# Second added exponential copies made on GpSimd as 32-bit additions, with planner limits every 20 units

## The chip, the cores and the metric

The kernel runs on one core of a Trainium2 chip. The metric is device time in microseconds: 1727.33 us is the median of three runs (1726.25 to 1729.32). The engines are called as in the profile: PE is TensorE's matrix multiplication and PEld its weight loads, DVE is VectorE, ACT is ScalarE, POOL is GpSimd, and SP issues the DMAs.

## The reference

Four attention layers in a row on x of 2048 tokens and 512 features, each with a layer norm ahead and a residual behind; the weights of the A layers are the same both times, and so are those of the B layers. There are 32 heads of 16 features.

```python
x = x + A(layernorm(x), wq, wk, wv, wo, beta)
x = x + B(layernorm(x), wqkv, wo)
x = x + A(layernorm(x), wq, wk, wv, wo, beta)
x = x + B(layernorm(x), wqkv, wo)

# B: full attention over all 2048 keys
scores = einsum('bhqd,bhkd->bhqk', q, k) * Dh ** (-0.5)
o = einsum('bhqk,bhkd->bhqd', softmax(scores), v) @ wo

# A: four segments of 512 tokens; causal attention inside a segment, and a memory of the earlier ones
p = softmax(q_s @ k_s.T * scale + mask); a_dot = p @ v_s
a_mem = (phi(q_s) @ M) / (phi(q_s) @ z + 1e-6)          # phi(t) = t + 1 if t > 0 else exp(t)
out_s = g * a_mem + (1 - g) * a_dot                     # g = sigmoid(beta)
M += phi(k_s).T @ v_s;  z += sum(phi(k_s))
```

## The kernel before

All of x stays in SBUF. The matrix of scores is never whole: a bank of PSUM (128 partitions by 512 float32) takes the scores of 128 keys against 512 queries of one head, and the exponential of the bank goes to SBUF as bf16. It is the weight of the next matmul (A layers) or its moving data (most of the B layers, called flipped: 17 columns of V and ones against 512 queries). The seventeenth column sums the exponentials, so that the normalisation comes after the PV product.

Work is a list of units. In each unit `unit` (L1650) issues the QK matmuls of three banks, or of two, and one ScalarE exponential over all of them (L1727, 1536 or 1024 elements per partition). Where a unit has only two banks for ScalarE, one or two more banks are given to VectorE: these are the taken banks (`dx_pick`, L1172). Every matmul goes through `mm` (L577), so the profile shows most of TensorE's work under that line.

VectorE makes its exponentials by arithmetic on bit patterns. `dx_first` (L1240, instruction at L1248) scales the scores from PSUM, adds a bias, and writes them as 16-bit integers, whose bits are then read as bf16. Two more copies of these codes, shifted by 36 and 84 (`EXP_STEPS`), are made from the first: the three values enter PV one after the other, and their sum approximates the exponential better than one. The added copies are instructions from SBUF to SBUF: `task_dx` (L1286) makes them over two banks, 1024 codes, at L1302; `dx_four` (L1309) does the same over four banks, 2048 codes, at L1319. The buffers are `dxt`, and KA, QA, VA, wA and wB once their own contents are no longer needed (`dx_buf`, L1196). That is why a copy appears in the profile as `VA<-KA` or `wB<-wB`.

Each taken bank therefore has three PV products in place of one. `pv_taken` (L1906) picks which of them TensorE issues after a unit, and `pv_phase` (L1926) issues them.

No order is left to the hardware: every engine has a queue that the program builds with its own clocks. `Sched.estimate` (L128) gives each instruction a planned end on its engine's clock from its inputs and a fixed duration; the planner compares these clocks (for example `late`, L1331) to decide whether to take a bank, when to run a background task (projections, layer norms, memory updates, the added copies), and what TensorE issues next. `held` and `PORT` there model that a VectorE operation from SBUF to SBUF waits for a GpSimd operation in progress. The limits of these decisions are class attributes of `Builder`; `PLAN` (L362) holds rows that replace some of them, one row for each stretch of `STRETCH` = 40 units (`set_limits`, L1972).

GpSimd's queue has, in the same planned order: the masking of diagonal blocks of the A layers (L1741), the multiplication that leaves one parity of heads in the queries (`qm`, L1617, `select` at L1575), the product by the reciprocal of the sums (`ob`, L1874, `divide` at L1864), some normalised x (`xn`, L777), and memsets. PSUM has eight banks: two slots of three for the units, and two for sums and background work.

Keep-warm matmuls with zeros are added to TensorE's list where it would otherwise be idle (`keep_busy`, L557, and `fill_gap`, L581).

Of the kernel before, what the change touches and what calls it, by code (L numbers as in the profile page):

```python
# [5 lines left out]
dt = mybir.dt  # L6
ACT = mybir.ActivationFunctionType
ALU = mybir.AluOpType

P = 128  # L10
# [77 lines left out]
class Sched:  # L88
# [4 lines left out]
    def __init__(self):  # L93
        self.ops = {e: [] for e in ENGS}
        self.t = {e: 0.0 for e in ENGS}
        self.tiles = []

        self.streams, self.cover = [], 0.0
        self.recent, self.over, self.pe_end, self.floor = [], [0.0, 0.0], 0.0, 0.0
        self.held, self.port, self.raw = [], False, False  # L100
        self.pe_seen, self.pe_no, self.pe_at = {}, [0], [0.0]
# [26 lines left out]
    def estimate(self, op, ns, gap, tile):  # L128
# [19 lines left out]
        elif e == "sp":  # L148
            st = max(ready, self.t[e])
            self.t[e] = st + max(gap, 600)  # L150
            op.end = st + ns
        else:
            op.end = max(self.t[e] + gap, ready + ns)
            if e == "pool":
                self.held = self.held[-7:] + [(op.end - ns, op.end)]
            elif self.port:
                for a, z in self.held:
                    if a + 20 < op.end - ns < z - PORT:
                        op.end = z - PORT + ns
            self.t[e] = op.end  # L160
# [198 lines left out]
class Builder:  # L359
    STRETCH = 40  # L360
# [3 lines left out]
        1: dict(ACT1=400, R_LATE=1200, DX_BANK=700, NEAR=18, FILL_DVE=400, BACK=3, CR_W=1900, CR_B=1800, R_PAIRS=2, PAIRS=24, DIV_LATE=800, DVE_LATE=800),  # L364
        2: dict(MARGIN=500, DX_BANK=900, NEAR=8, SLACK=550, EARLY=300, FILL=0.42, CR_B=1200, PART=3, NEARW=20, PAIRS=60, BUSY_WAIT=500, DX_FIN=3000, POOL_QM=1, POOL_XN=1),
        3: dict(ACT1=600, NEAR=8, TAKEN_A=1, SLACK=550, PV_SKIP=900, FILL_DVE=200, BACK=8, CR_W=1900, NEARW=20, OPART=2, TAKEN=0.4, LOW=14, DVE_LATE=800, QWAIT=8, HOLD_AT=40, PHI_LATE=0),
        4: dict(R_LATE=1200, NEARW=40, PAIRS=24, MASK_PE=800, LEVEL=3, TAKEN=0.5, LOW=30),
        5: dict(R_LATE=1500, DX_LATE=900, REST=12, NEAR=8, TAKEN_A=1, R_NEAR=50, PV_SKIP=500, FILL_DVE=400, BUSY_ROOM=900, CR_W=1300, DX_LAG=1, LOW=20, HOLD_SEGS=2),
        6: dict(ACT1=600, NEAR=10, PV_SKIP=200, DX_LAG=3, MASK_PE=800, LEVEL=3, DIV_LATE=2500, BG_BANK=100, QUAD=0),
        7: dict(ACT1=400, REST=16, NEAR=3, SLACK=350, R_NEAR=10, EARLY=0, FILL_DVE=200, BUSY_ROOM=300, CR_B=1800, R_PAIRS=2, PAIRS=999, TAKEN=0.3, QWAIT=8, QMIN=3, HOLD_AT=12, LN1_AT=6),  # L370
# [12 lines left out]
        20: dict(MARGIN=600, DX_LATE=900, EVAC_ACT=300, SLACK=550, PV_SKIP=100, CR_B=1200, R_PAIRS=2, MASK_PE=800, DIV_LATE=2500, BUSY_WAIT=500, GAP=1, BG_BANK=100, QWAIT=3, QMIN=3, HOLD_AT=40, LN1_AT=6, BUSY_BACK=800),
        21: dict(FILL_DVE=200, BACK=10, FILL=0.53, CR_W=1300, CR_B=1800, CR_A=1700, CARRY_W=0, NEARW=20, LEVEL=3, BG_BANK=400, QMIN=1, HOLD_MAX=0),
        22: dict(ACT1=200, DX_LATE=500, NEAR=10, PV_SKIP=200, EARLY=500, FILL=0.53, CR_B=1800, CARRY_W=1500, OPART=2, DX_LAG=1, MASK_PE=800, LEVEL=3, DIV_LATE=800, DVE_LATE=800, BG_BANK=100, QUAD=0, LN1_AT=6),
        23: dict(R_LATE=1200, R_NEAR=50, FILL_DVE=200, BACK=8, CR_A=1200, NEARW=40, OPART=4, PAIRS=999, LEVEL=3, TAKEN=0.25, QUAD=0, QMIN=4, HOLD_SEGS=2),
        24: dict(R_LATE=1500, DX_LATE=900, EVAC_ACT=100, REST=12, NEAR=8, TAKEN_A=1, SLACK=250, R_NEAR=50, PV_SKIP=100, EARLY=500, FILL_DVE=200, CR_W=1300, CR_A=1200, DX_LAG=1, LOW=20, BG_BANK=100, POOL_QM=1),
        25: dict(ACT1=300, MARGIN=600, R_LATE=2200, EVAC_ACT=1500, NEAR=18, CR_W=1900, CR_B=1800, R_PAIRS=2, DX_LAG=1, PAIRS=999, DIV_LATE=800, TAKEN=0.5, DVE_LATE=800, BG_BANK=400, PHI_LATE=300),
        26: dict(MARGIN=500, DX_LATE=700, REST=10, SLACK=350, EARLY=500, FILL_DVE=200, BUSY_ROOM=300, BACK=8, CR_W=1500, R_PAIRS=2, PAIRS=24, DIV_LATE=800, TAKEN=0.3, BG_BANK=100, QWAIT=8, QMIN=4, LN1_AT=6),
        27: dict(MARGIN=800, DX_BANK=700, REST=4, NEAR=10, SLACK=350, EARLY=500, FILL_DVE=200, BUSY_ROOM=300, BACK=8, CR_W=1500, PART=1, R_PAIRS=2, PAIRS=24, TAKEN=0.3, BG_BANK=100, QWAIT=8, QMIN=4, LN1_AT=6),  # L390
        28: dict(EVAC_ACT=800, NEAR=5, SLACK=350, R_NEAR=10, BACK=6, CARRY_W=400, NEARW=40, OPART=3, PAIRS=60, DIV_LATE=2500, BUSY_WAIT=0, TAKEN=0.3, DVE_LATE=800, BUSY_BACK=800),
        29: dict(DX_BANK=900, SLACK=700, PV_SKIP=100, EARLY=100, FILL_DVE=200, BUSY_ROOM=300, BACK=10, FILL=0.47, CR_W=1500, PART=3, R_PAIRS=2, TAKEN=0.3, DVE_LATE=800, LN1_AT=3, BUSY_BACK=800),
        30: dict(ACT1=300, MARGIN=800, REST=12, SLACK=700, PV_SKIP=100, EARLY=100, BACK=6, FILL=0.42, CR_W=1500, CARRY_W=400, PART=3, R_PAIRS=2, MASK_PE=800, DIV_LATE=2500, DVE_LATE=800, QWAIT=3, HOLD_MAX=0),
        31: dict(DX_LATE=700, DX_BANK=700, REST=20, PV_SKIP=100, BUSY_ROOM=900, FILL=0.57, CR_A=1700, PART=3, R_PAIRS=2, OPART=4, DX_LAG=3, MASK_PE=800, BUSY_WAIT=500, TAKEN=0.3, DVE_LATE=800, BG_BANK=100, QMIN=4, DX_FIN=3000),
# [891 lines left out]
    def task_dx(self):  # L1286
        while True:
# [18 lines left out]
            for i, (g, what, r) in enumerate(ents):  # L1306
                self.dxq.append((self.step + self.DX_LAG, g, what, r, b, i, [0]))
# [821 lines left out]
```

## Time and profile before

| | before |
|---|---|
| median of the runs | 1727.33 us (1726.25 to 1729.32, 3 runs) |
| span of the profiled execution, first to last instruction | 1724.4 us |
| ACT busy | 1696.4 us, 98% |
| PE busy | 1606.1 us, 93% |
| DVE busy | 1515.5 us, 88% |
| POOL busy | 211.3 us, 12% |
| granted TensorE clock, mean | 1.000 |

A group in the profile is named by line, engine, operation and tiles (`out<-in`, with the numbers of the buffers left out), then shapes and count, total busy time, mean duration of one in ns, and the idle time before it with what ended it. In a view by stretches each engine has its busy time in that stretch and, in brackets, its instructions; after the engines come the granted clock, the DMA share and GB/s. In a timeline the columns are start, duration, engine, line, operation. A row of waits reads: us in total, times, longest. Where one line of the program is shown alone, three durations are the shortest, median and longest one in ns.

### The profile page before, as it was taken

The numbers are of one execution on the slowest core, as the hardware profiler recorded it, in microseconds if no ns is written. First come the engines' busy times: TensorE is split into PE (matmuls) and PEld (weight loads), VectorE is DVE, ScalarE is ACT, GpSimd is POOL, SyncE is SP. The second block draws the span as 40 slices with busy tenths as digits, with TensorE's granted clock in tenths as the row PEclk, the third lists the DMA queues.
The fourth block names the chain that finished last, engine by engine and source line by source line (L and its number), as shares of the span: only waits on it lengthen the run. The fifth ranks groups of instructions, "written<-read, shape, count | busy, mean of one in ns | idle before, by whom it ended". The sixth has DMA issues, their size and how long they took to land.

```text
span 1724.4 us, 44750 instructions
## 1 busy us (share of the span) xinstructions
PE 1606.1 (93%) x19458; PEld 573.9 (33%) x19531; DVE 1515.5 (88%) x2928; ACT 1696.4 (98%) x1595; POOL 211.3 (12%) x321
## 2 busy tenths in 40 slices
PE   8898899999999899999999999999999999999999
PEld 4553435322222523522234222532222222222226
DVE  6757675999998789899886999889999999999997
ACT  8899999999999999999999999999999999999998
POOL 3211301111100402100002000110011000000000
PEclk9999999999999999999999999999999999999999
DMA  6110201000112131102112111011011000000000
GB/s 178 39 20 19 43 15 34 6 14 14 29 24 55 33 93 32 33 10 59 44 23 33 47 44 38 8 34 37 10 23 38 10 13 14 19 10 17 16 14 18
DMA packets 148421, 54.42 MB, mean 32 GB/s; under 512 B 128768, under 2 KB 147712, under 8 KB 148224
## 3 DMA queue, kind: packets, MB, share of 16 engines
q1 hardware_dynamic: 148224, 51.56, 13.9%
q8 instruction: 153, 2.51, 0.6%
q14 instruction: 44, 0.36, 0.1%
HBM read 18.88 MB, written 2.10 MB: 12 GB/s over the span
## 4 chain that ended last, share of the span: by engine, by line
ACT 77%; PE 16%; DVE 4%; issue 1%; POOL 1%; DMA 1%; another core or an unknown queue 0%; SPq 0%; ACTq 0%
ACT pT L1727 76%; PE ps L577 16%; ACT amem L844 1%; DVE lnst L748 1%; DVE KA L1248 0%; POOL xn L777 0%; DMA xT<-xn 0%; DVE wB L1248 0%; DMA tb<-ub 0%; DVE VA L639 0%; DVE lnst L750 0%; DVE KA L639 0%; DVE dxt L1248 0%; POOL qm L1617 0%; DVE wA L1248 0%
## 5 line engine op out<-in xcount | busy, mean ns | idle before, releaser
L1727 ACT ACTIVATE pT<-ps 128x1024 bf16<-128x1024 f32 (+1 forms) x1549 | 1664.6, 1280 | 15.5 <-PE ps L577 12.8
L577 PE MATMUL ps<-qm,KB 32*128 32x512 bf16 x4096 | 557.2, 384 | 78.1 <-ACT pT L1727 63.0
L577 PE MATMUL ps<-pT,VB 128*17 128x512 bf16 x2909 | 494.2, 384 | 2.0 <-DVE KA L1248 0.5
L577 PEld LDWEIGHTS ps<-qm,KB 32*128 32x128 bf16 x4096 | 143.4, 91 | 602.2 <-ACT pT L1727 515.1
L1248 DVE TENSOR_SCALAR KA<-ps 128x512 uint16<-128x512 f32 (+1 forms) x413 | 291.6, 723 | 11.2 <-PE ps L577 9.4
L1248 DVE TENSOR_SCALAR dxt<-ps 128x512 uint16<-128x512 f32 (+1 forms) x325 | 230.9, 721 | 14.0 <-PE ps L577 12.0
L577 PE MATMUL ps<-dxt,VB 128*17 128x512 bf16 x993 | 217.8, 381 | 0.0
L577 PEld LDWEIGHTS ps<-pT,VB 128*17 128x17 bf16 x2909 | 115.6, 87 | 285.2 <-issue 271.9
L1874 POOL TENSOR_TENSOR ob<-tb,rd 128x512 bf16<-128x512 bf16 x31 | 33.9, 1092 | 798.2 <-DVE rd L1870 798.2
L1248 DVE TENSOR_SCALAR wA<-ps 128x512 uint16<-128x512 f32 (+1 forms) x169 | 119.9, 723 | 2.3 <-PE ps L577 1.4
L577 PE MATMUL ps<-QA,VB 128*17 128x512 bf16 x420 | 117.8, 381 | 0.0
L1741 POOL TENSOR_SCALAR_AFFINE_SELECT pT<-pT 128x256 bf16<-128x256 bf16 (+4 forms) x128 | 67.4, 541 | 410.2 <-ACT pT L1727 410.2
L577 PE MATMUL ps<-woB,zero 128*32 128x512 bf16 (+1 forms) x347 | 115.1, 381 | 0.2 <-issue 0.2
L577 PE MATMUL ps<-VA,VB 128*17 128x512 bf16 x420 | 113.8, 381 | 0.0
L577 PE MATMUL ps<-wA,VB 128*17 128x512 bf16 x534 | 113.1, 381 | 0.0
L577 PE MATMUL ps<-qm,KA 32*128 32x128 bf16 (+2 forms) x1536 | 92.7, 254 | 18.0 <-ACT pT L1727 13.9
L1617 POOL TENSOR_SCALAR qm<-QB,par 128x512 bf16<-128x512 bf16 x98 | 79.0, 816 | 229.1 <-PE ps L577 215.8
L577 PE MATMUL ps<-VA,pT 128*128 128x51 bf16 (+1 forms) x2540 | 103.2, 187 | 1.8 <-DVE ob L1824 0.7
L577 PE MATMUL ps<-KA,VB 128*17 128x512 bf16 x420 | 100.7, 381 | 0.0
L577 PEld LDWEIGHTS ps<-VA,pT 128*128 128x128 bf16 x2540 | 88.7, 96 | 20.4 <-issue 7.7
L1302 DVE TENSOR_SCALAR dxt<-dxt 128x1024 uint16<-128x1024 uint16 (+1 forms) x216 | 85.7, 420 | 1.2
L1248 DVE TENSOR_SCALAR wB<-ps 128x512 uint16<-128x512 f32 (+1 forms) x108 | 84.1, 791 | 1.8 <-PE ps L577 0.8
(167 smaller groups left out, 1929.6 us busy)
## 6 DMA issues: line engine op xcount, KB each, us to landing
wB<-in_B_wqkv_dram SPq DMA_DIRECT2D x48, 128.0 KB, 2.3
wA<-in_A_wk_dram SPq DMA_DIRECT2D x16, 128.0 KB, 2.2
wA<-in_A_wq_dram SPq DMA_DIRECT2D x16, 128.0 KB, 2.3
wA<-in_A_wv_dram SPq DMA_DIRECT2D x16, 128.0 KB, 2.4
out_dram<-x SPq DMA_DIRECT2D x8, 256.0 KB, 2.2
x<-in_A_x_dram SPq DMA_DIRECT2D x3, 512.0 KB, 9.5
wB<-in_B_wqkv_dram SPq DMA_DIRECT2D x1, 1536.0 KB, 12.7
oT<-ob SPq DMA_TRANSPOSE x63, 2.5
```

Source lines behind the costliest of these rows:

```text
L577: self.sc.add("pe", lambda e: e.matmul(out, lhsT, rhs, start=start, stop=stop, skip_group_check=True), reads=reads, banks=[(bank, "w", all ...
L748: self.op("dve", (lambda i, t: lambda e: e.bn_stats(st[:, k, i, 0:6], self.x[:, t, :]))(i, t), reads=[self.b_x[t]], writes=[bs], ns=690, p ...
L844: self.op("act", lambda e: e.activation(et, src, ACT.Exp), reads=bsrc, writes=self.b_amem, ns=1023, gap=915)
L1248: self.op("dve", lambda e: e.tensor_scalar(d, o, SCALE * LOG2E * 128, 127.0 * 128 + EXP_BIAS, op0=ALU.mult, op1=ALU.add), writes=self.b_dx ...
L1302: self.op("dve", (lambda d, s, c: lambda e: e.tensor_scalar(d, s, float(c), None, op0=ALU.add))(d, s, c), reads=self.b_dxs[b][0:len(ents)] ...
L1617: self.op(eng, (lambda m, q, col: lambda e: e.tensor_scalar(m, q, col, 0.0, op0=ALU.mult, op1=ALU.add))(m, q, col), reads=[bq, self.b_par] ...
L1727: self.sc.add("act", (lambda dst, src: lambda e: e.activation(dst, src, ACT.Exp, scale=SCALE))(dst, src), writes=self.b_pT[slot * 3 + i:sl ...
L1741: self.op("pool", (lambda blk, pat: lambda e: e.affine_select(blk, blk, pattern=pat, compare_op=ALU.is_ge, fill=0.0, base=0, channel_multi ...
L1874: self.op(eng, lambda e: e.tensor_tensor(ob, t[:, :, :, 0:16], rb, ALU.mult), reads=[br] + self.b_tb, writes=self.b_ob[oi], **(dict(ns=125 ...
```

## The change

- The second added copy (shift 84) may be made by GpSimd. `pool_copy` views source and destination as 32-bit integers, two codes in each, and adds 84 × 65537, which shifts both halves by 84. The addend is one number per partition, in the new tile `shift`, read 512 times. Four banks at once become two such additions. The instruction depends on the source codes and on VectorE's first added copy of the same codes. It is put on GpSimd when GpSimd's planned clock is at most `POOL_C` (300) ns ahead of VectorE's; otherwise VectorE makes the copy as before.
- `dx_late` lets TensorE's list skip a PV product whose GpSimd copy is planned to come more than `POOL_WAIT` (100) ns after TensorE's clock. The product stays in the list for a later unit.
- The planned clock of GpSimd now also waits for VectorE operations from SBUF to SBUF in progress (`taken`).
- `STRETCH` is 20 in place of 40, and `PLAN` has 78 rows in place of 40, with other values.

```diff
     def estimate(self, op, ns, gap, tile):
...
             if e == "pool":
+                for a, z in self.taken:
+                    if a < op.end - ns + 20 < z:
+                        op.end = z - 20 + ns
                 self.held = self.held[-7:] + [(op.end - ns, op.end)]
             elif self.port:
                 for a, z in self.held:
                     if a + 20 < op.end - ns < z - PORT:
                         op.end = z - PORT + ns
+                self.taken = self.taken[-15:] + [(op.end - ns, op.end - 60)]
...
 class Builder:
-    STRETCH = 40
+    STRETCH = 20
     PLAN = {
...
+    POOL_C, POOL_NS, POOL_WAIT = 300, 2, 100
...
+        self.shift = sb("shift", [P, 1], dt.int32)
...
+        pool(lambda e: e.memset(self.shift[:, :], EXP_STEPS[1] * 65537), [self.b_shift])
...
     def task_dx(self):
...
                 d = self.dx_buf(b, k + 1)[:, 0:w]
+                if k and self.pool_copy(d, s, self.b_dxs[b][0:len(ents)], [self.b_dxt[b][k + 1]], self.b_dxt[b][k]):
+                    continue
...
+    def pool_copy(self, d, s, src, dst, first, now=False):
+
+        if not now and (not self.POOL_C or self.sc.t["pool"] > self.sc.t["dve"] + self.POOL_C):
+            return False
+        d, s = d.bitcast(dt.int32), s.bitcast(dt.int32)
+        n = 512 if len(src) == 2 else 256
+        c = bcast(self.shift[:, 0:1], [[0, n]])
+        self.op("pool", lambda e: e.tensor_tensor(d, s, c, ALU.add), reads=src + [first, self.b_shift], writes=dst, ns=150 + self.POOL_NS * n, gap=130 + self.POOL_NS * n)
+        self.cr_dve += 350
+        return True
...
     def dx_four(self, pairs):
...
+            d = self.dx_buf(b, k + 1, 2)
+            if k and self.pool_copy(d[:, 0:1024], s[:, 0:1024], self.b_dxs[b], [self.b_dxt[b][k + 1]], self.b_dxt[b][k]):
+                self.pool_copy(d[:, 1024:2048], s[:, 1024:2048], self.b_dxs[b + 1], [self.b_dxt[b + 1][k + 1]], self.b_dxt[b + 1][k], True)
+                self.cr_dve += 350
+                continue
             self.cr_dve -= 250
...
     def pv_taken(self, g, now, used=()):
...
             for ent in ents:
+                if not now and self.dx_late(ent):
+                    continue
                 if ent[6][0] <= len(EXP_STEPS) and loads[ent[3]] < level:
...
+    def dx_late(self, ent):
+
+        k, slot = ent[6][0], ent[4]
+        w = self.b_dxt[slot][k].last_write if 0 < k <= len(EXP_STEPS) else None
+        return w is not None and w.eng == "pool" and w.end + LAG["pool"] > self.sc.t["pe"] + self.POOL_WAIT
```

More of the change, by code (lines that the diff above doesn't have):

```diff
@@ L99, in __init__ @@
         self.recent, self.over, self.pe_end, self.floor = [], [0.0, 0.0], 0.0, 0.0
-        self.held, self.port, self.raw = [], False, False
+        self.held, self.taken, self.port, self.raw = [], [], False, False
         self.pe_seen, self.pe_no, self.pe_at = {}, [0], [0.0]
@@ L367 @@
[L367 to L370, printed above, removed]
@@ L402 @@
-        39: dict(R_LATE=2200, CR_W=1900, R_PAIRS=2, PAIRS=24, DIV_LATE=800),
+        1: dict(TAKEN_A=1, FILL_DVE=200, MASK_PE=800, PE_LOW=7, GAP=1, BG_BANK=400, QMIN=3, LOW=20),
+        2: dict(EVAC_ACT=800, NEAR=5, SLACK=350, R_NEAR=10, BACK=6, CARRY_W=400, NEARW=40, OPART=3, PAIRS=60, DIV_LATE=2500, BUSY_WAIT=0, TAKEN=0.3, DVE_LATE=800, BUSY_BACK=800, R_PAIRS=2),
+        3: dict(EVAC_ACT=800, NEAR=5, SLACK=350, R_NEAR=10, BACK=6, CARRY_W=400, NEARW=40, OPART=3, PAIRS=60, DIV_LATE=2500, BUSY_WAIT=0, TAKEN=0.3, DVE_LATE=800, BUSY_BACK=800, R_PAIRS=2, MARGIN=600),
@@ new lines @@
+        6: dict(ACT1=400, NEAR=8, TAKEN_A=1, SLACK=550, PV_SKIP=900, FILL_DVE=200, BACK=8, CR_W=1900, NEARW=20, OPART=2, TAKEN=0.4, LOW=14, DVE_LATE=800, QWAIT=8, HOLD_AT=40, PHI_LATE=0, REST=12),
+        7: dict(MARGIN=350, R_LATE=1500, DX_LATE=900, TAKEN_A=1, EARLY=300, CARRY_W=1500, PART=3, OPART=3, MASK_PE=800, GAP=3, QUAD=0, QWAIT=3, HOLD_SEGS=2, POOL_XN=1),
+        8: dict(R_LATE=1200, NEARW=40, PAIRS=24, MASK_PE=800, LEVEL=3, TAKEN=0.5, LOW=30, MARGIN=350, TAKEN_A=1, EARLY=300, OPART=3, QUAD=0, FILL=0.47, DX_BANK=900, CR_A=1200),
@@ new lines @@
+        9: dict(R_LATE=1200, NEARW=40, PAIRS=24, MASK_PE=800, LEVEL=3, TAKEN=0.5, LOW=30, MARGIN=350, TAKEN_A=1, EARLY=300, OPART=3, FILL=0.47, DX_BANK=900, CR_A=1200, HOLD_SEGS=2),
+        10: dict(ACT1=400, DX_BANK=700, NEAR=18, BACK=3, CR_W=1900, CR_B=1800, R_PAIRS=2, PAIRS=24, DIV_LATE=800, DVE_LATE=800),
+        11: dict(R_LATE=1500, DX_LATE=900, REST=12, NEAR=8, TAKEN_A=1, R_NEAR=50, PV_SKIP=500, FILL_DVE=400, BUSY_ROOM=900, CR_W=1300, DX_LAG=1, LOW=20, HOLD_SEGS=2, BACK=6),
+        12: dict(R_LATE=1500, DX_LATE=900, REST=12, NEAR=8, TAKEN_A=1, R_NEAR=50, PV_SKIP=500, FILL_DVE=400, BUSY_ROOM=900, CR_W=1300, DX_LAG=1, LOW=20, HOLD_SEGS=2, BACK=6, DVE_LATE=800, EARLY=500),
@@ new lines @@
+        13: dict(ACT1=600, NEAR=10, PV_SKIP=200, DX_LAG=3, MASK_PE=800, LEVEL=3, DIV_LATE=2500, BG_BANK=100, QUAD=0),
+        14: dict(ACT1=400, REST=16, NEAR=3, SLACK=350, R_NEAR=10, EARLY=0, FILL_DVE=200, BUSY_ROOM=300, CR_B=1800, R_PAIRS=2, PAIRS=999, TAKEN=0.3, QWAIT=8, QMIN=3, HOLD_AT=12, LN1_AT=6, CR_A=1200, MARGIN=500, DVE_LATE=800),
+        15: dict(MARGIN=400, NEAR=12, PV_SKIP=100, FILL_DVE=100, BUSY_ROOM=300, FILL=0.55, CR_W=1500, CARRY_W=400, R_PAIRS=2, OPART=3, GAP=3, DVE_LATE=800, QMIN=1, HOLD_AT=40, POOL_QM=1, PAIRS=24),
@@ new lines @@
+        19: dict(ACT1=400, DX_BANK=700, NEAR=18, BACK=3, CR_W=1900, CR_B=1800, R_PAIRS=2, PAIRS=24, DIV_LATE=800, DVE_LATE=800, POOL_C=1500),
+        20: dict(DX_BANK=900, SLACK=700, PV_SKIP=100, FILL_DVE=200, BUSY_ROOM=300, BACK=10, FILL=0.47, CR_W=1500, PART=3, R_PAIRS=2, TAKEN=0.3, DVE_LATE=800, LN1_AT=3, BUSY_BACK=800),
+        21: dict(DX_BANK=900, SLACK=700, PV_SKIP=100, FILL_DVE=200, BUSY_ROOM=300, BACK=10, FILL=0.47, CR_W=1500, PART=3, R_PAIRS=2, TAKEN=0.5, DVE_LATE=800, LN1_AT=3, BUSY_BACK=800, POOL_XN=1),
@@ new lines @@
+        34: dict(MARGIN=800, NEAR=5, SLACK=350, R_NEAR=10, PART=3, OPART=3, PAIRS=60, DIV_LATE=2500, TAKEN=0.4, DVE_LATE=1700, DX_FIN=3000, POOL_C=1),
+        35: dict(MARGIN=800, NEAR=5, SLACK=350, R_NEAR=10, PART=3, OPART=3, PAIRS=60, DIV_LATE=2500, TAKEN=0.4, DVE_LATE=800, POOL_QM=1),
+        36: dict(MARGIN=500, DX_LATE=700, REST=10, SLACK=350, EARLY=500, FILL_DVE=200, BUSY_ROOM=300, BACK=8, CR_W=1500, R_PAIRS=2, PAIRS=24, DIV_LATE=800, TAKEN=0.3, BG_BANK=100, QWAIT=8, QMIN=4, LN1_AT=6, NEAR=10, HOLD_SEGS=2, ACT1=600),
@@ new lines @@
+        37: dict(MARGIN=500, DX_LATE=700, REST=10, SLACK=350, EARLY=300, FILL_DVE=200, BUSY_ROOM=300, BACK=4, CR_W=1500, R_PAIRS=2, PAIRS=24, DIV_LATE=800, TAKEN=0.3, BG_BANK=100, QWAIT=8, QMIN=4, LN1_AT=6, NEAR=10, HOLD_SEGS=2, ACT1=600, CARRY_W=1500),
+        38: dict(MARGIN=800, NEAR=8, SLACK=350, R_NEAR=10, PART=3, OPART=3, PAIRS=60, DIV_LATE=2500, TAKEN=0.4, DVE_LATE=800),
+        39: dict(MARGIN=800, R_LATE=1200, DX_LATE=900, PV_SKIP=500, FILL_DVE=100, BACK=6, CR_B=1200, R_PAIRS=2, MASK_PE=800, DIV_LATE=2500, BUSY_WAIT=500, QWAIT=3, QMIN=4, R_NEAR=10, DVE_LATE=800, NEARW=20),
@@ new lines @@
+        46: dict(R_LATE=1200, NEAR=8, PV_SKIP=900, BUSY_ROOM=400, FILL=0.4, OPART=4, PAIRS=999, LEVEL=3, TAKEN=0.4, DVE_LATE=800, QWAIT=8, QMIN=3, BUSY_BACK=1800),
+        47: dict(MARGIN=350, R_LATE=1500, DX_LATE=900, TAKEN_A=1, CARRY_W=1500, PART=3, OPART=3, MASK_PE=800, GAP=3, QUAD=0, QWAIT=3, HOLD_SEGS=2, POOL_XN=1, POOL_WAIT=300),
+        48: dict(R_LATE=1500, DX_LATE=900, EVAC_ACT=100, NEAR=8, TAKEN_A=1, SLACK=250, R_NEAR=50, PV_SKIP=100, EARLY=500, FILL_DVE=200, CR_W=1300, CR_A=1200, DX_LAG=1, LOW=20, BG_BANK=100, POOL_QM=1, GAP=3, QWAIT=3, HOLD_SEGS=2, DVE_LATE=800),
@@ L403 @@
+        77: dict(DX_LATE=700, REST=8, SLACK=250, R_NEAR=20, CR_W=1300, R_PAIRS=2, NEARW=90, PAIRS=999, LEVEL=1, LOW=20, GAP=1, DVE_LATE=800, BG_BANK=400, QUAD=0),
     }
```

85 lines of the change are left out of this document (51 added, 34 removed).

## The prediction

> **What bounds the kernel now.** I read the page's head and its chain first, then the busy time of each engine by stretch, then who waits for whom.
>
> ```profile
> span 1724.4 us, 44750 instructions
> PE 1606.1 (93%) x19458; PEld 573.9 (33%) x19531; DVE 1515.5 (88%) x2928; ACT 1696.4 (98%) x1595; POOL 211.3 (12%) x321
> ACT 77%; PE 16%; DVE 4%; issue 1%; POOL 1%; DMA 1%; another core or an unknown queue 0%; SPq 0%; ACTq 0%
> ```
>
> ACT works 1696.4 of 1724.4 us and carries 77% of the chain, so the end is ACT's work plus 28.0 us in which it idles. The stretches say where it idles, and how full the other engines are there.
>
> ```profile
> core 0: us, PE busy (x) PEld busy (x) DVE busy (x) ACT busy (x) POOL busy (x), PEclk, DMA share, GB/s
> 0.00:172.00 172.00, 151.76 (x2202) 79.05 (x2229) 116.19 (x282) 155.91 (x130) 37.65 (x81) 1.00 0.26 64
> 172.00:300.00 128.00, 116.27 (x1632) 52.50 (x1644) 83.07 (x184) 126.56 (x99) 22.04 (x30) 1.00 0.17 30
> 300.00:500.00 200.00, 189.31 (x2032) 55.36 (x2032) 191.56 (x369) 199.19 (x196) 27.92 (x38) 1.00 0.09 17
> 500.00:700.00 200.00, 186.58 (x2348) 71.16 (x2357) 169.53 (x364) 198.63 (x182) 35.57 (x47) 1.00 0.24 51
> 1300.00:1500.00 200.00, 188.09 (x1896) 49.48 (x1893) 197.72 (x314) 199.91 (x207) 17.12 (x19) 1.00 0.09 20
> 1500.00:1700.00 200.00, 188.75 (x2217) 59.05 (x2214) 197.44 (x312) 199.87 (x201) 12.18 (x13) 1.00 0.07 14
> 1700.00:1724.00 24.00, 20.18 (x424) 13.30 (x423) 12.25 (x28) 18.51 (x19) 0.00 (x0) 1.00 0.07 24
> ```
>
> Of ACT's idle, 16.1 us lie before 172 us and 5.5 us in the tail; between them it misses some 6 us only. From 1300 to 1700 us VectorE is as full as ACT (395.2 of 400 us): there every bank moved from ACT needs VectorE time that doesn't exist. POOL has 88% of its time free.
>
> ```profile
> ACT pT L1727 <- PE ps L577: 12.8, 32, 1.3
> PE ps L577 <- ACT pT L1727: 76.9, 269, 1.1
> ```
>
> TensorE waits 76.9 us for ACT to free banks, and ACT only 12.8 us for TensorE: TensorE has some 77 us of slack.
>
> **ACT: what is removed.** The instruction orders of the two programs have 1015 exponentials of 1024 elements before and 1024 after, and 534 of 1536 before and 516 after. That is 3632 banks (2×1015 + 3×534) against 3596: 36 more banks go to VectorE. The copies that ACT makes at L637 stay nine in number. Exponentials overlap their predecessors, so the step is taken from rows that are nearly all of one width, beside the mean durations:
>
> ```profile
> L1727 ACT ACTIVATE pT<-ps 128x1024 bf16<-128x1024 f32 x1015 | 982.6, 1144 | 1.2 <-PE ps L577 0.4
> L1727 ACT ACTIVATE pT<-ps 128x1536 bf16<-128x1536 f32 x534 | 771.2, 1538 | 14.3 <-PE ps L577 12.4
> 1371.30 26.98 ACT L1727 ACTIVATE pT<-ps 128x1024 bf16<-128x1024 f32 x29
> 589.45 12.23 ACT L1727 ACTIVATE pT<-ps 128x1536 bf16<-128x1536 f32 x9
> ```
>
> A short one costs (26.98 − 1.14)/28 = 0.92 us, a long one (12.23 − 1.54)/8 = 1.34 us. The change is 9×0.92 − 18×1.34 = −15.8 us. By the groups' busy time (0.968 and 1.444 each) it would be −17.3 us, which counts overlaps twice; I take −15.8.
>
> **VectorE: what is removed and added.** Each bank that VectorE takes needs one read of PSUM (L1248) and two added copies from it (L1302, or L1319 for four banks at once).
>
> ```profile
> L1302 DVE TENSOR_SCALAR dxt<-dxt 128x1024 uint16<-128x1024 uint16 x200 | 81.6, 430 | 1.2
> L1302 DVE TENSOR_SCALAR VA<-KA 128x1024 uint16<-128x1024 uint16 x114 | 49.2, 431 | 0.0
> L1319 DVE TENSOR_SCALAR dxt<-dxt 128x2048 uint16<-128x2048 uint16 x70 | 48.1, 700 | 0.3
> L1319 DVE TENSOR_SCALAR VA<-KA 128x2048 uint16<-128x2048 uint16 x53 | 36.4, 687 | 0.0
> L1248 DVE TENSOR_SCALAR KA<-ps 128x512 uint16<-128x512 f32 x382 | 254.5, 683 | 9.7 <-PE ps L577 8.2
> L1248 DVE TENSOR_SCALAR KA<-ps 128x1024 uint16<-128x1024 f32 x31 | 37.9, 1221 | 1.5 <-PE ps L577 1.2
> ```
>
> Over all tiles, copies of 1024 go from 544 to 352 (−192 × 0.43 = −83 us), copies of 2048 from 274 to 141 (−133 × 0.69 = −92 us), copies of 512 from 24 to 34 (+10 × under 0.43, taken as +3 us). Reads of one bank go from 926 to 908 (−18 × 0.683 = −12 us), reads of two from 89 to 116 (+27 × 1.221 = +33 us). Together −151 us: VectorE falls from 1515 to about 1364 us, before it waits for anything new. What hides its longer list of banks is thus the time of its own copies; if that cover is gone, see the rivals.
>
> **GpSimd: what is added.** 482 additions of 512 code pairs and 14 of 256: about 85% of all second copies (570 pairs of banks). No row has a 32-bit addition of two operands on POOL. The nearest are these:
>
> ```profile
> L1874 POOL TENSOR_TENSOR ob<-tb,rd 128x512 bf16<-128x512 bf16 x31 | 33.9, 1092 | 798.2 <-DVE rd L1870 798.2
> L1617 POOL TENSOR_SCALAR qm<-QB,par 128x512 bf16<-128x512 bf16 x98 | 79.0, 816 | 229.1 <-PE ps L577 215.8 <-DVE QB L639 13.3
> L777 POOL TENSOR_SCALAR xn<-x,lnst,lnw 128x512 bf16<-128x512 bf16 x8 | 17.4, 2177 | 19.5 <-DVE lnw L768 18.1 <-DMA xT<-xn 1.3
> ```
>
> The bounds are 0.82 us (one streamed operand) and 2.18 us; I take 1.09 us, since L1874 is the same operation on as many elements with two streamed operands. POOL grows by 482×1.09 + 14×0.6 = 534 us to about 745 us, 44% of the span. With 2.18 us it would be at 1270 us, still short of the span. The Trainium skill ("GPSIMD Engine Reference", Elementwise — side-by-side cycle accounting) gives 4497 ns for a float32 tensor_tensor of 2048 elements; a quarter, 1.12 us as an estimate, would put POOL at 760 us, and no run here shows it for integers.
>
> Additions stand in POOL's queue behind a wait for VectorE's first copy. Behind them wait the masks of L1741 (for TensorE's PV), the qm of L1617 (for the next group's QK) and the normalising product of L1874 (for a DMA transpose and the output projection). None is moved to another queue, and the DMA issues stay 353 on SP.
>
> **The port.** A VectorE copy from SBUF to SBUF is held while POOL is in an instruction:
>
> ```profile
> 1403.93 1.06 POOL L1874 TENSOR_TENSOR ob<-tb,rd 128x512 bf16<-128x512 bf16 x1 [37.77 <-DVE rd L1870]
> 1404.42 1.11 DVE L1319 TENSOR_SCALAR wB<-wB 128x2048 uint16<-128x2048 uint16 x1
> 1404.96 1.80 POOL L1617 TENSOR_SCALAR qm<-QB,par 128x512 bf16<-128x512 bf16 x2
> 1406.25 1.06 DVE L1319 TENSOR_SCALAR wB<-wB 128x2048 uint16<-128x2048 uint16 x1
> L1319 DVE TENSOR_SCALAR wB<-wB x48: 632/684/1115, 400.9 to 1647.0; 128x2048 uint16<-128x2048 uint16 x48
> L1302 DVE TENSOR_SCALAR VA<-KA x118: 285/418/964, 314.0 to 1708.9; 128x1024 uint16<-128x1024 uint16 x114, 128x512 uint16<-128x512 uint16 x4
> ```
>
> Both copies take 1.1 us in place of the median 0.684, and end about 0.55 us after the POOL operation they met. Low bound of the loss: today the means exceed the medians by some 12 ns (430 and 431 against 418, 700 and 687 against 684), 10 us over 818 copies, with 211 us of POOL; 3.5 times the POOL work on 527 copies gives 10×3.5×527/818 = 22 us. High bound: about 670 VectorE operations from SBUF to SBUF, each starting at random against a POOL that is busy 44% of the time, with half of a 1.09 us addition to wait: 160 us. I take 50 us, nearer the measured end but above it, since an addition starts right behind a copy and so near the next ones. VectorE then stands at 1364 + 50 = 1414 us, 83% of the span against 88% now. Even with 160 us it is at 1524 us, where it is today, so the ACT saving survives both ends.
>
> **TensorE.** Each of the 36 banks needs three PV matmuls in place of one. A PV costs 113.8/420 = 0.27 us of TensorE's time by its group, so 72 more are 20 us at most; the matmuls with zeros that keep TensorE occupied cost 115.1/347 = 0.33 us, and their 32-column form falls from 395 to 322, −24 us. The two cancel, and either alone lies inside the 77 us of slack.
>
> ```profile
> L577 PE MATMUL ps<-VA,VB 128*17 128x512 bf16 x420 | 113.8, 381 | 0.0
> L577 PE MATMUL ps<-woB,zero 128*32 128x512 bf16 (+1 forms) x347 | 115.1, 381 | 0.2 <-issue 0.2
> ```
>
> New are the waits: about 430 PV matmuls of the changed program wait on POOL for a copy. Queued behind such a PV, in order, are the next QK matmuls, and ACT waits for those. Today's price of the same wait on VectorE's copies is the last row here, for L1319:
>
> ```profile
> L1319 DVE TENSOR_SCALAR VA<-KA x53: 671/683/948, 407.2 to 1678.8; 128x2048 uint16<-128x2048 uint16 x53
> ...
> who waited for it (us, times):
>   PEld ps L577: 1.3, 3
> ```
>
> 1.3 us in three waits over 274 copies is some 2.5 us over 496 additions if POOL's copies come as punctually. It may be zero inside TensorE's slack; I pass it to ACT in full: +2.5 us.
>
> **The sum** against the profiled execution: 1724.4 − 15.8 + 2.5 = 1711.1 us of span. The median of the runs is 1727.33, 2.9 us above that span, so 1714 us. The forecast's own range is 1707 to 1721: down by ACT's other price (1.5 us) and some of the 21 us that ACT idles at both ends, which the new limits also rearrange; up by several such waits.
>
> **Rivals.** *POOL late, TensorE stalls* (slower). The planner lets TensorE take a POOL-made copy when it is due within 0.1 us, so lateness goes straight into TensorE's in-order queue. For it: three engines' jitter now meets in one chain (copy, addition, PV), and an addition can itself be held by a VectorE copy of 0.43 or 0.69 us. Against it: the rows just shown, three waits in 274. With a mean lateness x the stall is 430x; the first 77 us vanish in slack, 16 us more eat the gain, so it decides from x = 93/430 = 0.22 us. If every addition starts half a VectorE copy late (352 of 0.43 and 141 of 0.69 us, mean 0.50), x is 0.25 us: 430×0.25 − 77 = 31 us, and 1727 − 16 + 31 = 1742 us.
>
> *The port serialises VectorE* (slower). The Trainium skill speaks against the change: "Perfetto Trace Analysis", Optimizing Scalar/DVE Operations, says that the two engines share a port under an exclusive lock, so that offloading from one to the other might not help; the held copies above agree with the lock. Worked from the rows: if each meeting costs a whole addition, 670×0.44×1.09 = 321 us, VectorE has 1364 + 321 = 1685 us. The 395 us it works from 1300 to 1700 would become 439, 39 us too many: 1727 − 16 + 39 = 1750 us. Against it: measured losses are at the 22 us end.
>
> *Given back* (no change). The present plan leaves ACT idle 6 us from 172 to 1700 us, a very close packing of 40 rows of limits. New limits every 20 units need only pack 16 us worse, 1% of that stretch, and the saved exponentials turn into waits on TensorE: 1727 us. For it: at 172 to 300 TensorE is at 91% and VectorE at 65%, so there VectorE's relief buys nothing.
>
> **Chances.** Forecast 0.64; given back 0.13 (0.03 of it still faster, 0.08 the same, 0.02 slower); POOL late 0.17; port 0.06. A change under 0.2% (3.5 us) can't be told from none. Faster 0.67, the same 0.08, slower 0.25. The range that should hold the time 8 times in 10 is 1704 to 1740: the forecast's range, the given-back case, and the near side of the two slow ones.
>
> **What would show it.** ACT's groups should show 1024 and 516 exponentials and about 1681 us busy; VectorE 1390 to 1450 us; the additions near 1.1 us each. In the waits, TensorE on POOL should be under 10 us in total; tens of us there, with ACT idle behind it, is the first rival. VectorE copies averaging 0.7 us for 1024 elements, and a full VectorE, are the second. ACT idle growing by 15 us with POOL punctual is the third. I'm wrong in the first term if ACT's busy time falls by clearly less than 15 us, and in the price of the addition if it runs near 2 us.

## The result, and the profile after

The changed kernel takes 1720.23 us in the median of four runs (1720.08 to 1720.49), against 1728.14 us for the kernel before beside it. The ratio is 0.9958 with a 95% interval of 0.9945 to 0.997: 0.4% faster. One of the four runs of oldplan, below, took 1783.92 us at a granted clock of 0.855 where the other three had 0.998 and more, and isn't counted. The forecast was 1714 us with a range of its own of 1707 to 1721.

The page of the changed kernel, head and chain, in the columns shown for before:

```profile
span 1718.4 us, 45396 instructions
PE 1610.9 (94%) x19708; PEld 578.9 (34%) x19775; DVE 1460.6 (85%) x2623; ACT 1681.9 (98%) x1586; POOL 736.1 (43%) x825
ACT 67%; PE 17%; DVE 13%; issue 1%; DMA 1%; POOL 1%; SPq 0%; another core or an unknown queue 0%; ACTq 0%; DVEq 0%
```

ACT's work fell by 14.5 us (1696.4 to 1681.9) and the span by 6.0 us, so ACT's idle time grew from 28.0 to 36.5 us. VectorE lost 55 us of work, yet its share of the chain went from 4% to 13%. POOL grew by 525 us. The stretches say where ACT idles now:

```profile
core 0: us, PE busy (x) PEld busy (x) DVE busy (x) ACT busy (x) POOL busy (x), PEclk, DMA share, GB/s
300.00:500.00 200.00, 191.12 (x2030) 54.89 (x2027) 182.65 (x312) 199.44 (x197) 102.20 (x111) 1.00 0.12 25
...
1100.00:1300.00 200.00, 188.03 (x2258) 65.26 (x2259) 165.65 (x280) 194.72 (x180) 87.17 (x108) 1.00 0.12 25
1300.00:1500.00 200.00, 187.50 (x1920) 48.53 (x1917) 193.03 (x289) 198.45 (x209) 122.06 (x119) 1.00 0.09 20
1500.00:1700.00 200.00, 189.86 (x2309) 61.93 (x2307) 189.92 (x277) 197.87 (x203) 111.86 (x107) 1.00 0.06 14
1700.00:1718.00 18.00, 14.11 (x302) 9.39 (x303) 2.26 (x5) 10.38 (x10) 0.00 (x0) 1.00 0.10 32
```

From 1300 to 1700 us ACT misses 3.7 us where it missed 0.2, though VectorE now has 17 us to spare there. Five more are missing from 1100 to 1300 us, where VectorE is at 83%; p16 below, which has the same queues and short additions, still misses 3.5 us there, so the larger part of these five belongs to the new order of work. In neither stretch is it a full VectorE that ACT waits for. The waits name what came late. First the changed kernel, then the same kinds of row of the kernel before (us in total, times, longest):

```profile
ACT pT L1790 <- PE ps L622: 19.8, 49, 1.4
ACT oT L1183 <- PE ps L657: 4.5, 1, 4.5
PE ps L622 <- ACT pT L1790: 57.0, 211, 1.0
PE ps L622 <- DVE dxt L1294: 3.6, 9, 0.7
PE ps L622 <- DVE wB L1294: 3.0, 7, 0.7
PE ps L622 <- DVE KA L1294: 2.7, 8, 0.7
PE ps L622 <- DVE wA L1294: 0.8, 3, 0.3
PE ps L622 <- POOL VA L1364: 1.0, 1, 1.0
```

```profile
PE ps L577 <- DVE wB L1248: 1.7, 4, 0.7
PE ps L577 <- DVE KA L1248: 1.3, 3, 0.5
PE ps L577 <- DVE dxt L1248: 0.6, 2, 0.4
PE ps L577 <- DVE wA L1248: 0.5, 2, 0.3
```

TensorE waits 10.1 us, 27 times, for VectorE's reads of PSUM (L1294, formerly L1248); it was 4.1 us, 11 times. It waits 1.0 us for an addition of GpSimd, and 0.3 us for GpSimd's masks (0.7 before). So GpSimd's results come in time, and what comes late is VectorE giving PSUM banks back. The groups show why (mean ns of one after the comma):

```profile
L1790 ACT ACTIVATE pT<-ps 128x1024 bf16<-128x1024 f32 x1024 | 980.8, 1130 | 5.3 <-PE ps L622 4.1
L1790 ACT ACTIVATE pT<-ps 128x1536 bf16<-128x1536 f32 x516 | 736.8, 1511 | 17.0 <-PE ps L622 15.8
L1364 POOL TENSOR_TENSOR VA<-KA,shift 128x512 int32<-128x512 int32 x190 | 198.2, 1053 | 229.4 <-DVE QA L1350 143.1 <-DVE QA L1382 80.7 <-DVE lnw L812 2.9
L1350 DVE TENSOR_SCALAR QA<-KA 128x1024 uint16<-128x1024 uint16 x120 | 58.5, 489 | 1.2
L1350 DVE TENSOR_SCALAR wB<-wB 128x1024 uint16<-128x1024 uint16 x62 | 38.2, 629 | 0.6
L1382 DVE TENSOR_SCALAR QA<-KA 128x2048 uint16<-128x2048 uint16 x52 | 41.6, 801 | 0.6
```

VectorE's remaining copies became slower: 489 to 629 ns where 430 was usual, 801 ns in place of some 690. One chain of it, in the timeline of the changed kernel:

```profile
1675.54 2.04 POOL L1364 TENSOR_TENSOR wB<-wB,shift 128x512 int32<-128x512 int32 x2
1676.75 1.38 DVE L1382 TENSOR_SCALAR dxt<-dxt 128x2048 uint16<-128x2048 uint16 x1
1678.05 1.27 DVE L1294 TENSOR_SCALAR wA<-ps 128x512 uint16<-128x512 f32 x2
1678.78 0.39 PE L622 MATMUL ps<-qm,KB 32*128 32x512 bf16 x2 [0.35 <-DVE wA L1294]
1680.15 1.97 ACT L1790 ACTIVATE pT<-ps 128x1024 bf16<-128x1024 f32 x2 [0.65 <-PE ps L622]
```

Two additions occupy GpSimd until 1677.58. The copy that VectorE starts at 1676.75 takes 1.38 us in place of 0.684 and ends 0.55 us after them. The read of PSUM behind it is late, the QK matmul into that bank waits 0.35 us, and the QK matmuls of the next unit stand behind it in TensorE's queue: ACT pauses 0.65 us.

### The profile page after: what moved, and what is told of

Read it like the earlier page. It is cut to its first block, busy times and chain, and to the rows that moved or that the text cites. A ratio compares the mean times of both kernels' runs of the same rounds, so it can differ in the third digit from the quotient of the medians.

```text
span 1718.4 us, 45396 instructions
## 1 busy us (share of the span) xinstructions
PE 1610.9 (94%) x19708; PEld 578.9 (34%) x19775; DVE 1460.6 (85%) x2623; ACT 1681.9 (98%) x1586; POOL 736.1 (43%) x825
## 4 chain that ended last, share of the span: by engine, by line
ACT 67%; PE 17%; DVE 13%; issue 1%; DMA 1%; POOL 1%; SPq 0%; another core or an unknown queue 0%; ACTq 0%; DVEq 0%
ACT pT L1790 65%; PE ps L622 17%; DVE dxt L1294 2%; DVE KA L1294 1%; DVE wA L1294 1%; ACT amem L890 1%; DVE wB L1294 1%; DVE QA L1382 1%; DVE lnst L794 1%; POOL xn L823 0%; SPq L691 0%; DVE wA L1382 0%; DVE dxt L1382 0%; DVE dxt L1350 0%; DMA xT<-xn 0%
## 5 line engine op out<-in xcount | busy, mean ns | idle before, releaser
L1294 DVE TENSOR_SCALAR KA<-ps 128x512 uint16<-128x512 f32 (+1 forms) x396 | 291.9, 757 | 14.8 <-PE ps L622 11.8
L1364 POOL TENSOR_TENSOR VA<-KA,shift 128x512 int32<-128x512 int32 (+1 forms) x193 | 200.1, 1047 | 231.0 <-DVE QA L1350 144.6
L1364 POOL TENSOR_TENSOR dxt<-dxt,shift 128x512 int32<-128x512 int32 (+1 forms) x143 | 149.3, 1052 | 282.9 <-DVE dxt L1350 197.5
L1294 DVE TENSOR_SCALAR dxt<-ps 128x512 uint16<-128x512 f32 (+1 forms) x307 | 218.9, 729 | 19.2 <-PE ps L622 17.6
L1294 DVE TENSOR_SCALAR wB<-ps 128x512 uint16<-128x512 f32 (+1 forms) x171 | 122.7, 733 | 5.1 <-PE ps L622 4.0
L622 PE MATMUL ps<-wB,VB 128*17 128x512 bf16 x534 | 124.2, 381 | 0.0
L1364 POOL TENSOR_TENSOR wA<-wA,shift 128x512 int32<-128x512 int32 (+1 forms) x78 | 81.5, 1057 | 99.5 <-DVE wA L1350 65.2
L622 PE MATMUL ps<-KA,VB 128*17 128x512 bf16 x430 | 113.8, 381 | 0.0
L1294 DVE TENSOR_SCALAR wA<-ps 128x512 uint16<-128x512 f32 (+1 forms) x150 | 108.2, 741 | 2.8 <-PE ps L622 2.3
L1364 POOL TENSOR_TENSOR wB<-wB,shift 128x512 int32<-128x512 int32 (+1 forms) x82 | 87.0, 1070 | 51.7 <-DVE wB L1350 33.7
L622 PE MATMUL ps<-woB,zero 128*32 128x512 bf16 (+1 forms) x307 | 102.4, 380 | 0.2
```

Source lines behind the costliest of these rows:

```text
L622: self.sc.add("pe", lambda e: e.matmul(out, lhsT, rhs, start=start, stop=stop, skip_group_check=True), reads=reads, banks=[(bank, "w", all ...
L1294: self.op("dve", lambda e: e.tensor_scalar(d, o, SCALE * LOG2E * 128, 127.0 * 128 + EXP_BIAS, op0=ALU.mult, op1=ALU.add), writes=self.b_dx ...
L1364: self.op("pool", lambda e: e.tensor_tensor(d, s, c, ALU.add), reads=src + [first, self.b_shift], writes=dst, ns=150 + self.POOL_NS * n, g ...
```

## The experiments

All but nopool, oldplan and split2b have the queues of the changed kernel, instruction for instruction on TensorE, VectorE, ScalarE and SP, so that only what GpSimd's additions cost or when they start differs. The theory, called "port" in the expectations: additions keep VectorE's copies out, these delay its reads of PSUM, and TensorE's queue passes that on to ACT. Rivals: the new limits pack ACT less tightly whatever an addition costs ("packing", the given-back case of the prediction), and GpSimd's copies come too late ("POOL late").

**p16 and p256: shorter additions.** The edit of p16; p256 has 256 in place of 16.

```diff
+        m = n * 16 // 512
+        dd, ss, cc = d[:, 0:m], s[:, 0:m], bcast(self.shift[:, 0:1], [[0, m]])
-        self.op("pool", lambda e: e.tensor_tensor(d, s, c, ALU.add), reads=src + [first, self.b_shift], writes=dst, ...
+        self.op("pool", lambda e: e.tensor_tensor(dd, ss, cc, ALU.add), reads=src + [first, self.b_shift], writes=dst, ...
...
     def pv_phase(self, ent):
...
-        self.pv(g, what, r, self.dx_buf(slot, k)[:, 512 * i:512 * i + 512].bitcast(dt.bfloat16), self.b_dxt[slot][k] if k else self.b_dxs[slot][i])
+        w = self.b_dxt[slot][k].last_write if k else None
+        kk = 1 if w is not None and w.eng == "pool" else k
+        self.pv(g, what, r, self.dx_buf(slot, kk)[:, 512 * i:512 * i + 512].bitcast(dt.bfloat16), self.b_dxt[slot][k] if k else self.b_dxs[slot][i])
...
```

> The queues of all engines are those of the changed kernel; each addition covers 16 of its 512 code pairs, and the third PV product reads the first added copy in its place (so the output is another one). From the 0.61 us of 256 pairs and the 1.04 us of 512 an addition should take about 0.21 us. Theory 'port': VectorE's copies held behind additions make its PSUM reads late, TensorE's queue waits for them, and that is where ACT's idle time between 172 and 1690 us comes from (14.4 us against 5.9 before). Then holds nearly vanish, this idle falls to 6 us and the time to about 1712 us. Rival 'packing': the new limits simply pack ACT less tightly, whatever an addition costs; then the idle stays at 12 to 15 us and the time at 1719 to 1721 us.

> As p16 with 256 of 512 pairs, 0.61 us each. Port: about half of the way, idle of some 9 us and 1715 to 1717 us. Packing: 1719 to 1721 us, as the changed kernel.

p16 took 1709.59 us (ratio 0.9892, interval 0.9877 to 0.9908), p256 1709.45 us (0.9895, 0.9881 to 0.9908). Busy time, ACT's wait, TensorE's waits for reads of PSUM, the additions (shortest/median/longest in ns) and one stretch of p16, then busy time of p256:

```profile
PE 1608.3 (94%) x19775; PEld 575.3 (34%) x19775; DVE 1407.0 (82%) x2623; ACT 1678.2 (98%) x1586; POOL 324.6 (19%) x825
ACT pT L1792 <- PE ps L622: 14.4, 34, 1.4
PE ps L622 <- DVE wB L1294: 0.9, 2, 0.4
PE ps L622 <- DVE dxt L1294: 0.6, 2, 0.4
PE ps L622 <- DVE KA L1294: 0.4, 1, 0.4
L1366 POOL TENSOR_TENSOR VA<-KA,shift x193: 198/211/646, 307.2 to 1674.6; 128x16 int32<-128x16 int32 x190, 128x8 int32<-128x8 int32 x3
1100.00:1300.00 200.00, 188.47 (x2262) 64.00 (x2260) 161.07 (x283) 196.45 (x183) 43.14 (x107) 1.00 0.13 25
```

```profile
PE 1607.1 (94%) x19775; PEld 574.8 (34%) x19775; DVE 1419.0 (83%) x2623; ACT 1678.5 (98%) x1586; POOL 522.2 (31%) x825
```

Packing is out: with the same queues the time falls by 10.6 us against 1720.23, so with additions of 0.21 us the plan would be worth some 18 us. ACT's idle time from 172 to 1690 us is 7.7 us, close to the 6 expected. VectorE executes the same 2623 instructions in 1407.0 us in place of 1460.6, so full additions cost it 53.6 us more than short ones. The traces show which instructions pay: by count times mean duration over all groups, VectorE's copies take 263.0 us in p16 and 313.2 us in the changed kernel, its reads of PSUM 763.1 and 760.0. The copies are held, and the reads are only late: TensorE waits 1.9 us for them, 5 times, in place of 10.1 us, 27 times. The expectation of half the way for p256 was wrong: additions of 0.61 us cost VectorE 12 us more than those of 0.21, and no time at all. So the first 12 us of VectorE's loss were free in these queues, and 54 us were not.

**p768: longer additions, and later copies.**

```diff
+        op, h = self.sc.ops["pool"][-1], n // 2
+        d2, s2, c2 = d[:, 0:h], s[:, 0:h], bcast(self.shift[:, 0:1], [[0, h]])
+        new = Op("pool", 0, lambda e: e.tensor_tensor(d2, s2, c2, ALU.add))
+        new.deps = list(op.deps)
+        op.deps = op.deps + [new]
+        self.sc.ops["pool"].insert(len(self.sc.ops["pool"]) - 1, new)
```

> The same queues, but ahead of each addition GpSimd makes its first half once more, and the addition waits for that: about 1.7 us in place of 1.04 us for each copy, POOL 1070 us or so busy. Port: VectorE's losses to holds rise from 67 to about 110 us, ACT idles 10 us more, 1728 to 1735 us. Packing: 1719 to 1722 us. Rival 'POOL late' of the prediction: copies come 0.7 us later, TensorE waits tens of us for POOL itself, 1740 us and more; if TensorE's waits for POOL stay under 10 us, there was a reserve of that size and this rival was far away.

It took 1783.91 us (1.0325, 1.0311 to 1.0339). Busy time, TensorE's waits for additions, and ACT's wait:

```profile
PE 1649.2 (92%) x19775; PEld 586.2 (33%) x19775; DVE 1497.1 (84%) x2623; ACT 1692.2 (95%) x1586; POOL 1061.6 (59%) x1321
PE ps L622 <- POOL wA L1364: 9.5, 8, 2.9
PE ps L622 <- POOL dxt L1364: 8.8, 12, 2.9
PE ps L622 <- POOL VA L1364: 8.3, 9, 2.7
PE ps L622 <- POOL wB L1364: 5.1, 7, 1.0
ACT pT L1796 <- PE ps L622: 72.4, 122, 3.7
```

Here the POOL-late rival is real: TensorE waits 31.7 us for additions, and VectorE loses 36.5 us more than in the changed kernel (1497.1 − 1460.6). Both act at once, so the 64 us can't be divided between them. The changed kernel's copies have less than 0.7 us of reserve.

**nofirst: the addition doesn't wait for VectorE's first copy.**

```diff
...
+        op = self.op("pool", lambda e: e.tensor_tensor(d, s, c, ALU.add), reads=src + [first, self.b_shift], writes=dst, ...
+        op.deps = [w for w in op.deps if w is not first.last_write] + [x.last_write for x in src]
...
```

> The same queues; the addition no longer waits for VectorE's first added copy, only for the codes that it reads. It can then take the port ahead of that copy. Port: a good part of the 493 copies is held for most of an addition, some 0.5 us each, VectorE loses 150 us or more to holds in place of 67, 1740 to 1780 us. Packing: 1718 to 1722 us, since POOL's results only come earlier.

It took 1740.59 us (1.0074, 1.0062 to 1.0087):

```profile
PE 1632.4 (94%) x19775; PEld 582.9 (34%) x19775; DVE 1485.5 (85%) x2623; ACT 1687.0 (97%) x1586; POOL 787.9 (45%) x825
```

Additions that may start earlier make the kernel 20 us slower, because they now overtake the copies: VectorE's copies take 342.7 us by count times mean (313.2 in the changed kernel), and TensorE waits 19.6 us, 48 times, for reads of PSUM; no matmul waits for an addition. VectorE loses 24.9 us more than in the changed kernel, a good deal less than the expected 80 and more, and yet the time is at the near end of the expected 1740 to 1780 us. The order "behind VectorE's copy" is worth 1.2% here.

**split2, split2r, split4: the same addition in pieces.** The edit of split2; split4 has n // 4.

```diff
+        h, op = n // 2, self.sc.ops["pool"].pop()
+        for i in range(0, n, h):
+            di, si, ci = d[:, i:i + h], s[:, i:i + h], bcast(self.shift[:, 0:1], [[0, h]])
+            fn = (lambda di, si, ci: lambda e: e.tensor_tensor(di, si, ci, ALU.add))(di, si, ci)
...
+        self.sc.ops["pool"].append(op)
```

> The queues of the changed kernel, but each addition is two instructions of half the code pairs, one behind the other: 2 x 0.61 us in place of 1.04 us, POOL some 820 us busy. A VectorE copy can come between the two halves. Theory 'port, by the length of one hold': what hurts is the longest time for which one instruction keeps a copy out, so holds shrink to about those of 0.61 us and the time falls to 1711 to 1716 us. Rival 'port, by the total': the port's total time counts, and it is 17% longer, so VectorE loses more and the time is 1722 to 1735 us. If lateness of the copies themselves counted, TensorE would wait for POOL by some us more, since they end 0.2 us later.

split2 took 1715.13 us (0.9931, 0.9919 to 0.9944). It was run once more beside the changed kernel on one chip, with a split into four:

> The changed kernel again, beside split2r on the same chip: 1719 to 1722 us.

> split2 again. If two halves are better than one addition, 1713 to 1717 us, and its interval lies clear of that of after2; if the difference was the chip's, the two overlap.

> Four instructions of 128 pairs for each addition, about 4 x 0.40 = 1.6 us for a copy in place of 1.04, with VectorE kept out for 0.4 us at a time. Theory 'length of one hold': VectorE's losses fall further, but copies come 0.55 us later, so that TensorE now waits for POOL itself; with the 0.7 us later copies of p768 that cost far more than the holds, so 1725 to 1770 us, and TensorE's waits for POOL at 10 to 30 us. If only holds counted, 1710 to 1714 us.

After2 took 1721.09 us (0.9958, 0.9945 to 0.9972), split2r 1715.50 us (0.9926, 0.9914 to 0.9939), split4 1729.85 us (1.0011, 1.0002 to 1.0019). Busy time of split2r, then of split4 with TensorE's waits for additions there:

```profile
PE 1607.0 (94%) x19708; PEld 577.1 (34%) x19775; DVE 1440.9 (84%) x2623; ACT 1681.0 (98%) x1586; POOL 826.9 (48%) x1321
```

```profile
PE 1612.6 (93%) x19708; PEld 578.3 (33%) x19775; DVE 1435.0 (83%) x2623; ACT 1682.4 (97%) x1586; POOL 985.3 (57%) x2313
PE ps L622 <- POOL wA L1368: 4.5, 6, 1.2
PE ps L622 <- POOL VA L1368: 4.2, 5, 2.8
PE ps L622 <- POOL dxt L1368: 1.9, 3, 1.4
PE ps L622 <- POOL wB L1368: 1.2, 3, 0.5
```

In two halves GpSimd is busy 90 us longer than in the changed kernel, VectorE 20 us shorter, and the kernel is faster than both the one before and the changed one, by 0.7% and 0.3%. A copy in halves comes some 0.2 us later (2 × 0.61 us against 1.04), and in the changed kernel TensorE waits just 1.0 us for additions: that the copies of p16 and p256 come earlier can explain little of their gain. So how long one instruction keeps a copy out counts for more than GpSimd's total. It isn't all that counts: p256 has one instruction of 0.61 us for each copy where split2r has two, and split2r is 6 us slower, with 292.1 us of VectorE's copies (273.9 in p256), 4.9 us of TensorE's waits for reads of PSUM (2.8) and 1.7 us of its waits for additions (none). In four pieces VectorE gains 6 us more, but copies come later still, TensorE waits 11.8 us for additions, and the gain is gone.

**nopool and oldplan: additions off, and limits of before.**

```diff
 nopool
...
-            setattr(self, name, self.PLAN.get(k, {}).get(name, getattr(type(self), name)))
+            setattr(self, name, 0 if name == "POOL_C" else self.PLAN.get(k, {}).get(name, getattr(type(self), name)))
...
 oldplan
-    STRETCH = 20
+    STRETCH = 40
     PLAN = {
...
```

> The changed kernel with GpSimd's additions switched off in the planner (POOL_C is 0 everywhere), the 78 rows of limits kept: VectorE makes all copies, and the planner lays the queues anew. If the rows by themselves carried the gain, 1715 to 1722 us; if they only fit the queues with GpSimd's additions, clearly slower than before, 1735 us or more, with VectorE at 88% or more and ACT idle tens of us.

> GpSimd's additions with the 40 rows of limits of before (each for 40 units), laid anew by the planner. If the additions by themselves carried the gain, below 1727 us; if limits only fit the queues that they were chosen for, slower than before, 1735 us or more, although VectorE has less to do.

nopool took 1753.94 us (1.0156, 1.0142 to 1.017), oldplan 1745.96 us in the median of three (1.0114, 1.0095 to 1.0132). In oldplan the rows of PLAN are those of the kernel before. In both the planner lays all queues anew. Their busy times:

```profile
PE 1643.0 (94%) x19682; PEld 584.1 (33%) x19682; DVE 1504.1 (86%) x2862; ACT 1703.3 (97%) x1584; POOL 228.9 (13%) x331
```

```profile
PE 1629.5 (93%) x19693; PEld 578.6 (33%) x19693; DVE 1451.1 (83%) x2636; ACT 1698.6 (97%) x1598; POOL 719.9 (41%) x821
```

Either half of the change alone makes the kernel slower, by 1.6% and 1.1%. The limits fit the queues for which they were chosen, and so the gain can't be divided between GpSimd's help and the finer limits. How far rows every 20 units would go for VectorE alone wasn't tried on the chip and stays open.

**split2b: split2 with values of the limits chosen again.**

> split2 with some of the 78 rows of limits chosen again, so that the planned end is 0.7 us earlier. If the plan's clocks hold, 1713 to 1716 us; the queues differ, so that holds fall elsewhere, and 1712 to 1720 us would not surprise.

It took 1715.21 us (0.9929, 0.9917 to 0.9942), the same as split2.

## Why the prediction was right, and where it was off

**The direction and the size** came out within the forecast's own range; the span is 7.3 us above the 1711.1 predicted for it. Of these, 1.3 us are ACT's work (14.5 us less in place of 15.8) and 6.0 us are ACT's idle time, which grew by 8.5 us where 2.5 were allowed.

**ACT's term** was −15.8 us and measured −14.5 us (1681.9). With short additions it is −18.2 us (p16, 1678.2). The term depends on the pauses: the end of an exponential is covered by the next one unless ACT pauses, and ACT paused for TensorE 49 times in the changed kernel and 34 times in p16. Fifteen pauses of 1.14 − 0.92 = 0.22 us make 3.3 of these 3.7 us, as an estimate. That 14.5 lies so near to 15.8 is partly luck: p16 pauses about as often as the kernel before (34 and 32 times), and its 18.2 us are nearer to the 17.3 that the prediction set aside.

**The additions** cost 1.05 to 1.08 us in the mean of a tile's group where 1.09 was taken, and POOL is busy 736 us where 745 was forecast. TensorE's wait for them is 1.0 us where 2.5 us was allowed. POOL late didn't happen; its reserve is measured from the other side, by split4 and p768.

**VectorE's relief** was mis-sized: 1414 us were forecast and 1460.6 measured, with the holds sized about rightly at 50 us (53.6 us between p16 and the changed kernel). Already p16, whose additions are five times shorter, has 1407 us where 1364 was forecast. Removed copies were priced at full duration, but neighbours overlap, as two rows of the changed kernel show:

```profile
1336.43 0.41 DVE L1350 TENSOR_SCALAR wA<-wA 128x1024 uint16<-128x1024 uint16 x1
1336.76 0.41 DVE L1350 TENSOR_SCALAR QA<-KA 128x1024 uint16<-128x1024 uint16 x1
```

The second starts 0.33 us after the first, so a copy in such a row is worth 0.33 us and not 0.41. That is nearly the whole 43 us: from the kernel before to p16, VectorE's instructions by count times mean fell by 150.1 us (1688.9 to 1538.8), as priced (151), and its busy time by 108.5 us, because 41.6 us of overlap went with them.

**The step that failed** is the one on the port: "Even with 160 us it is at 1524 us, where it is today, so the ACT saving survives both ends." The size of the holds was about right, their price was not zero. It was judged by VectorE's total, and the total doesn't decide: one copy held 0.7 us makes one read of PSUM late, and TensorE's queue is in order. The sum's only term for waits, +2.5 us, was for waits on POOL; those that came were on VectorE's reads. The runs put the price of full additions at 10.6 us (1720.23 against 1709.59; of ACT's idle time 6.5 us, 36.5 against 30.0), and that is what separates the 18 us that the plan would be worth with short additions from the 8 us that were had. The second rival had this mechanism, with its decision placed at a full VectorE; it takes its price far earlier, with VectorE 85% busy in the mean and 97% from 1300 to 1500 us. The Trainium skill's caution ("Perfetto Trace Analysis", Optimizing Scalar/DVE Operations) that such an offload might not help is borne out in part: the held copies took 10.6 of 18 us, and 0.4% was left.

## What to carry to other kernels

When work goes from VectorE to GpSimd, look at how long a single GpSimd instruction keeps VectorE's copies out and at what stands behind those copies, not at the sum of busy times: here, with the same queues, one instruction of 0.61 us for each copy cost nothing, two of 0.61 us cost 6 us and one of 1.04 us cost 10.6 us. Put the GpSimd instruction behind the VectorE copy from the same source (20 us here), and split it in two if its result has time to spare (four pieces lost all of the gain here). A set of scheduling limits was fitted here to one way of making the copies; one half of such a change, tried alone, told little about its worth.

## What the runs showed of the hardware that was not expected

A 32-bit addition of two streamed operands on GpSimd took 0.21 us for 16 pairs per partition, 0.61 us for 256 and 1.04 us for 512: 0.185 us and 1.66 ns a pair. It is no dearer than the product of two 16-bit operands (1.06 us at its shortest for 512), so a code pair costs what a single code does. The float32 row of the Trainium skill used in the prediction (an estimate of 1.12 us from "GPSIMD Engine Reference", Elementwise — side-by-side cycle accounting) is 8% above the integer addition measured here.

With the same queues of TensorE, VectorE and ScalarE, the order of the times is that of the sum of both waits (but for p16 and p256, which are equal), and not that of VectorE's busy time: split4 has VectorE less busy than split2r and takes 14 us more. Copies are count times mean over VectorE's exponential copies from SBUF to SBUF; the waits are sums of the rows of TensorE's matmuls; all in us:

| run | VectorE busy | its copies | TensorE waits for reads of PSUM | for additions | time |
|---|---|---|---|---|---|
| p16 | 1407.0 | 263.0 | 1.9 | 0 | 1709.59 |
| p256 | 1419.0 | 273.9 | 2.8 | 0 | 1709.45 |
| split2r | 1440.9 | 292.1 | 4.9 | 1.7 | 1715.50 |
| changed kernel | 1460.6 | 313.2 | 10.1 | 1.0 | 1720.23 |
| nofirst | 1485.5 | 342.7 | 19.6 | 0 | 1740.59 |
| split4 | 1435.0 | 287.8 | 3.1 | 11.8 | 1729.85 |
| p768 | 1497.1 | 347.4 | 18.1 | 31.7 | 1783.91 |
